# Inverting the first four units' triangles on TensorE by repeated squaring, in a fused recurrence and feed-forward kernel

## The chip, the cores and the metric

The kernel runs on one core of a Trainium2 chip. The metric is the device time of one execution in microseconds, as the median of several executions. The engines of a core are named as the profile names them: PE (TensorE), DVE (VectorE), ACT (ScalarE), POOL (GpSimd) and SP (which issues most transfers).

## What is computed

A recurrence over 768 time steps for 4 x 8 heads of width 40, and then a feed-forward layer with hard-swish over the 3072 tokens of width 320. All data are float32, except that the two weight matrices come as float64.

```python
for t in range(S):
    y[:, :, t] = np.einsum('bhd,bhde->bhe', rt, state)
    Sa = np.einsum('bhde,bhe->bhd', state, at)
    state_decay = state * wt[:, :, None, :] - np.einsum('bhd,bhe->bhde', Sa, bt)
    state = state_decay + np.einsum('bhd,bhe->bhde', vt, kt)
# x: y as (3072 tokens, 320)
h = x @ w_in                                  # 320 -> 2048
g = h * np.clip(h + 3.0, 0.0, 6.0) / 6.0
out = g @ w_out                               # 2048 -> 320
```

The kernel takes time in blocks of 64 steps. A *unit* is one block of two batch entries with their eight heads, so there are 24 units, in *groups* of four (two blocks of the two pairs of batch entries). In a block the recurrence becomes products of matrices, and it needs, for each head, the inverse of a 64 x 64 triangular matrix with ones on the diagonal, made from the products of a and b.

## The kernel before

What matters here is in four parts. Names: `NU` is 4 units, `H` 8 heads, `BL` 64 steps, `L` 32, `NH` = 32 heads of a group.

Preparation of a unit has nine stages: W and gam (decay products), A, B, K (turned and scaled), F (the triangles), factor (`KBt`), E (the masked scores) and EV. A unit's own step has RT, R, VT, S, U, C, UT, rS, sn, H, y and the moves that hand its rows to the feed-forward part.

The inversion of a whole group is done by VectorE on 32 x 32 blocks, in place, with the heads on partitions. It takes 30 rounds of a product and an addition, and the next round needs the one before it.

```python
def invert(F, third, alone=False):
    fb = inv.tile([P, L, L], F32, name="fb")
    nc.vector.transpose(out=fb..., in_=F[:, :, 0:L]...)
    x = inv.tile([P, L, L], F32, name="x", tag="x", bufs=1)
    nc.gpsimd.affine_select(out=x[:], in_=fb[:], ...)
    ...
    for i in range(1, L - 1):
        nc.vector.tensor_tensor(out=pv, in0=..., in1=..., op=ALU.mult)     # prod
        yield
        nc.vector.tensor_tensor(out=rest, in0=rest, in1=pv, op=ALU.add)    # x
        yield
    tb = ...;  nc.vector.transpose(out=tb..., in_=x[:])
    tt = ...;  nc.vector.transpose(out=tt..., in_=x...)
    third.append((F, tb, tt))
```

The third 32 x 32 block of each 64 x 64 inverse is then made on TensorE from `tb`, `tt` and `F`, for two units at a time, and the inverse lies in `tinv`:

```python
def third_block(F, tb, tt, n, first=False):
    for h in range(2 * H):
        for x in range(2):
            nc.tensor.matmul(out=zp[x]..., lhsT=F[...], rhs=tb[...])
    ... # zs <- zp on ScalarE; with first, tinv <- tb on GpSimd
    for h in range(2 * H):
        for x in range(2):
            nc.tensor.matmul(out=tp[x]..., lhsT=tt[...], rhs=zs[...])
    ... # tinv <- tp on ScalarE
```

`U` and `UT` are the first stages that need `tinv`:

```python
def s_U():
    ...
    nc.tensor.matmul(out=up[x]..., lhsT=tinv[half(x), n * H + 4 * s + pr, :], rhs=m["R"]...)
```

The weights arrive as float64 in 20 pieces, and are converted to float32 by VectorE and ScalarE in five steps for each piece. A step is taken each time the generator is advanced; the raw pieces lie in tiles that are not needed yet, among them those of the inversion (`x`, `fb`, `tt`).

```python
def load_weights():
    ...
    for n in range(PIECES + 1):
        nc.vector.tensor_scalar(x, hi, 20, 0x7FF, ...)              # parts
        nc.scalar.activation(out=x, in_=x, func=AF.Relu, ...)       # parts
        yield
        nc.vector.scalar_tensor_tensor(m, raw..., 2.0 ** -52, m, ...)   # of the piece before
        yield
        nc.vector.tensor_tensor(out=out, in0=m, in1=yf, op=ALU.mult)    # win, win2 or wout
        yield
        nc.vector.scalar_tensor_tensor(x, hi, 0x80000000, x, ...)
        yield
        nc.vector.tensor_scalar(hi, hi, 0xFFFFF, 0x4B000000, ...)
        nc.scalar.activation(out=m, in_=m, func=AF.Copy, ...)
        yield
```

The feed-forward part is a stream of jobs, each half of the hidden width for one unit: `expand` (products with `win`, then hard-swish into `gt`) and `contract` (products with `wout`). The first jobs of units 0 and 1 can begin when ten pieces are converted, and all others need all 20:

```python
def available():
    i, r = jobs[0]
    return i in ready and converted[0] >= (PIECES // 2 if i < SPLIT and r == 0 else PIECES)
```

The prelude prepares units 0 to 3 in pairs, starts the inversion of all four at once, advances the weights and some early stages beside it, and then runs the units by a plan:

```python
for t, _ in enumerate(by_twos(0, 4, MIXED, 0, {5: 1, 6: 1, 10: 1})):
    ...
while not third:                 # the inversion of the first group
    aside(1)
    if n % 3 == 1:
        next(weights, None)
    if n % EARLY == 0 and early:
        run(early.popleft())
firsts = [third_block(*third[-1], n, True) for n in (0, 2)]
run(firsts[0]); run(firsts[0], weight=1)
PLAN = """0 U 0 UT 1 R
          0 sn 0 H T
          1 U 1 UT 0 y
          ... """                # T: third block of units 2 and 3
```

After the prelude a steady loop runs the other 20 units, each group with `invert`, `third_block` and the feed-forward jobs in between. The whole kernel:

Of the kernel before, what the change touches and what calls it, by code (L numbers as in the profile page):

```python
# [8 lines left out]
F32 = mybir.dt.float32  # L9
# [7 lines left out]
P = 128  # L17
BL = 64
# [11 lines left out]
def kernel(  # L30
# [111 lines left out]
    mask4 = _ap(mask[:], 0, [[0, 4], [1, BL]])  # L142
    three = const.tile([P, 1], F32, name="three")
# [37 lines left out]
    for name in "BK":  # L181
        others[name] = second(name)
# [44 lines left out]
    def raw_homes():  # L227
# [16 lines left out]
        order = [g, h, a, b, c, d, e, f, a, b, c, d, "x", "fb", "tt", a, b, "fb", "tt", a]  # L244
        free = [None] * 8 + [2, 3, 4, 5, None, None, None, 8, 9, 13, 14, 15]
# [205 lines left out]
    def prepare(i, F):  # L451
# [42 lines left out]
        def b_stage():  # L494
            x = turn_pairs(o["BN"])
            yield PE
            bt = o["bt"] = turned("bt")
            nc.vector.tensor_tensor(out=bt[:], in0=x[:], in1=o["rg"][:], op=ALU.mult)
# [110 lines left out]
    def invert(F, third, alone=False):  # L609
# [26 lines left out]
        if not alone:  # L636
            yield
# [5 lines left out]
        if alone:  # L643
            return
# [6 lines left out]
    def third_block(F, tb, tt, n, first=False):  # L651
# [3 lines left out]
        parts = [slice(0, H), slice(H, 2 * H)] if first else [slice(0, 2 * H)]  # L655
# [8 lines left out]
        for part in parts:  # L664
            for x in range(2):
                z = x * BL
                nc.scalar.activation(out=zs[z:z + L, part], in_=zp[x][z:z + L, part], func=AF.Copy)
        if first:
            for part in parts:
                heads = slice(n * H + part.start, n * H + part.stop)  # L670
                for z in range(0, P, BL):
                    nc.gpsimd.tensor_copy(tinv[z:z + L, heads, 0:L], tb[z:z + L, heads])
                    nc.gpsimd.tensor_copy(tinv[z + L:z + BL, heads, L:BL], tb[z + L:z + BL, heads])
# [9 lines left out]
        for part in parts:  # L683
            heads = slice(n * H + part.start, n * H + part.stop)
            for x in range(2):
                z = x * BL
                nc.scalar.activation(out=tinv[z:z + L, heads, L:BL], in_=tp[x][z:z + L, part],
                                     func=AF.Copy)
# [331 lines left out]
    RFETCH, EARLY, MIXED = 8, 5, 1 / 3  # L1020
    TWOS = 14

    def by_twos(first, steps, mixed, rate, fill={}):
# [3 lines left out]
        for t in range(TWOS):  # L1027
# [8 lines left out]
            if t == 10:  # L1036
                side.append(invert(group_F[-1], third, first == 0))
            yield


    ring.clear()
    ring.extend([("any", 5)] * 5 + [("h", 2)] * 2)
    for name in "WABK":
        for i, engine in enumerate((nc.sync, nc.scalar if name == "W" else nc.sync)):
            fetch(name, i, engine)
    for t, _ in enumerate(by_twos(0, 4, MIXED, 0, {5: 1, 6: 1, 10: 1})):
        if t == 0:
            next(weights)
        limit[0] = {7: 4, 10: 12}.get(t, limit[0])
        while t == 7 and refill[0]():  # L1050
            pass
        if t == RFETCH:
            fetch("R", 0)
    ring.clear()
    ring.append(("any", 5))
    blocks = {}


    stages = [step(i) for i in range(NU)]
    chains = [in_turn(stages[0], ["RT", "VT", "C", "R"]), in_turn(stages[1], ["RT", "VT", "C"])]  # L1060
    early = deque(chains[i] for i in (0, 0, 1, 1, 0, 1, 0))
    n, cleared = 0, []
    while not third:
        aside(1)
        if not third:
            n += 1
            if n % 3 == 1:
                next(weights, None)
            if converted[0] == 2 and not cleared:
                cleared.append(nc.gpsimd.memset(tinv[:], 0.0))  # L1070
# [221 lines left out]
```

## Time and profile before

| | |
|---|---|
| time, median of 3 | 856.66 us (855.93 to 857.93) |
| span of the profiled execution | 853.2 us |
| PE busy | 774.1 us (91%), 15480 instructions |
| DVE busy | 529.4 us (62%), 1032 instructions |
| ACT busy | 310.1 us (36%), 756 instructions |
| POOL busy | 157.5 us (18%), 307 instructions |
| chain that ended last | PE 78%, DVE 12%, issue 3% |

The profile divides the span into 40 slices of 21.3 us and gives the busy share of each engine in each slice as a digit (9 is 90% or more), so that the stages can be told apart. Matmuls of float32 leave two records for each instruction of the program, and transposes leave one. A line of a timeline gives the start, the duration, the engine, the line of the kernel and the operation, and in brackets the idle time before it with what ended it.

### The profile page before, as it was taken

To read this page: it belongs to the slowest core of one execution; us is meant where nothing else is said; L and a number is where in the kernel's file an instruction comes from. 1 tells how busy PE (TensorE), PEld (TensorE's weight loads), DVE (VectorE), ACT (ScalarE), POOL (GpSimd) and SP (SyncE) were. 2 spreads that over 40 slices of the span, in tenths; PEclk is the share of its full clock that TensorE was granted. 3 is DMA by queue.
4 is the path that set the end of the run, shared out by engine and by line. 5 is a ranking of instruction groups with operands and counts; after the bars stand their busy time and mean duration, and the time that the engine had idled before them with its cause. 6 is when DMAs were issued, how large, how long until landed. Compare 5 with 4: busy or idle time off the path is not lost.

```text
span 853.2 us, 34881 instructions
## 1 busy us (share of the span) xinstructions
PE 774.1 (91%) x15480; PEld 660.0 (77%) x15480; DVE 529.4 (62%) x1032; ACT 310.1 (36%) x756; POOL 157.5 (18%) x307
## 2 busy tenths in 40 slices
PE   4723877898999989999999999999999999999998
PEld 3622766776888878888888888888888888888886
DVE  6988598878864579734698454697445674221211
ACT  1322654231344433444324534334453324222111
POOL 3231212112121130221211122113012202000000
PEclk9755878899999999999999999999999999999999
DMA  7572443331123330322231232222232101110000
GB/s 137 86 181 80 112 113 80 64 57 24 33 49 67 59 62 11 61 50 46 46 56 29 43 66 49 45 42 39 41 55 50 18 20 27 25 22 12 17 18 15
DMA packets 174213, 44.99 MB, mean 53 GB/s; under 512 B 157424, under 2 KB 172784, under 8 KB 174064
## 3 DMA queue, kind: packets, MB, share of 16 engines
q1 hardware_dynamic: 171920, 42.44, 26.0%
q8 instruction: 122, 2.00, 1.0%
q10 hardware_dynamic: 2144, 0.33, 0.2%
q14 instruction: 27, 0.22, 0.1%
HBM read 34.08 MB, written 3.93 MB: 45 GB/s over the span
## 4 chain that ended last, share of the span: by engine, by line
PE 78%; DVE 12%; issue 3%; ACT 2%; POOL 1%; DMA 1%; SPq 0%; DVEq 0%; ACTq 0%
PE o L945 24%; PE h L921 20%; PE any L420 6%; PE h L926 5%; PE any L438 3%; PE any L841 3%; PE any L818 3%; DVE prod L626 2%; PE any L660 2%; PE any L679 2%; DVE x L632 2%; PE any L763 2%; PE any L784 1%; PE any L725 1%; PE any L583 1%
## 5 line engine op out<-in xcount | busy, mean ns | idle before, releaser
L945 PE MATMUL o<-wout,gt 128*128 128x320 f32 x768 | 234.8, 449 | 0.0
L921 PE MATMUL h<-xt,win 128*128 128x128 f32 x1536 | 197.6, 283 | 3.2 <-DVE gt L932 3.2
L921 PEld LDWEIGHTS h<-xt,win 128*128 128x128 f32 x1536 | 186.4, 196 | 12.1 <-DVE gt L932 3.9
L945 PEld LDWEIGHTS o<-wout,gt 128*128 128x128 f32 x768 | 139.2, 191 | 54.3 <-issue 1.2
L932 DVE SCALAR_TENSOR_TENSOR gt<-gt,h 128x512 f32<-128x512 f32 x96 | 61.4, 681 | 95.4 <-ACT gt L931 95.4
L931 ACT ACTIVATE gt<-h,three 128x512 f32<-128x512 f32 x96 | 60.8, 684 | 128.0 <-PE h L926 127.8
L856 POOL TENSOR_TENSOR yg<-ys,gam 128x512 f32<-128x512 f32 x24 | 41.3, 1723 | 212.5 <-DVE ys L853 153.9
L626 DVE TENSOR_TENSOR prod<-x 128x30 f32<-128x30 f32 (+9 forms) x180 | 64.1, 356 | 13.4 <-POOL x L617 8.1
L632 DVE TENSOR_TENSOR x<-x,prod 128x30 f32<-128x30 f32 (+9 forms) x180 | 63.9, 355 | 5.5 <-DVE prod L626 0.3
L556 POOL TENSOR_TENSOR KBt<-K,rgt 128x320 f32<-128x320 f32 x24 | 21.6, 899 | 221.6 <-ACT rgt L548 216.3
L926 PE MATMUL h<-xt,win 64*128 64x128 f32 x768 | 55.8, 285 | 0.0
L447 DVE COPY_PREDICATED score<-mask,any 128x256 f32<-128x256 int32 x143 | 53.2, 434 | 1.1 <-PE any L438 1.1
L926 PEld LDWEIGHTS h<-xt,win 64*128 64x128 f32 x768 | 46.6, 187 | 5.2 <-issue 0.3
L474 DVE RECIPROCAL gam<-prods 128x256 f32<-128x256 f32 x24 | 41.5, 1741 | 13.4 <-POOL yg L856 13.1
L825 DVE TENSOR_TENSOR state<-any,state 128x160 f32<-128x160 f32 x48 | 13.3, 319 | 56.0 <-PE any L438 54.5
L489 DVE RECIPROCAL rgam<-prods 128x256 f32<-128x256 f32 x24 | 41.8, 1741 | 0.0
L589 ACT ACTIVATE EV<-any 64x160 f32<-64x160 f32 x92 | 24.8, 295 | 44.4 <-PE any L583 32.6
L463 DVE TENSOR_TENSOR_SCAN prods<-wm,start 128x528 f32<-128x528 f32 x24 | 30.1, 1253 | 16.6 <-ACT wm L460 15.0
L853 DVE TENSOR_TENSOR ys<-any,ys 128x256 f32<-128x256 f32 x44 | 16.6, 418 | 34.5 <-PE any L583 19.9
L704 ACT ACTIVATE RT<-any 128x512 f32<-128x512 f32 x24 | 14.3, 595 | 59.4 <-PE any L420 59.4
L841 PE MATMUL any<-score,KBt 64*64 64x64 f32 x1536 | 31.4, 230 | 2.7 <-DVE score L447 1.6
L841 PEld LDWEIGHTS any<-score,KBt 64*64 64x64 f32 x1536 | 27.3, 142 | 7.6 <-issue 3.3
(184 smaller groups left out, 1137.7 us busy)
## 6 DMA issues: line engine op xcount, KB each, us to landing
B<-in_b_dram SPq DMA_DIRECT2D x48, 80.0 KB
K<-in_k_dram SPq DMA_DIRECT2D x48, 80.0 KB
V<-in_v_dram SPq DMA_DIRECT2D x96, 40.0 KB
out_dram<-ob SPq DMA_DIRECT2D x48, 80.0 KB
R<-in_r_dram SPq DMA_DIRECT2D x92, 40.0 KB
W<-in_w_dram SPq DMA_DIRECT2D x40, 80.0 KB
A<-in_a_dram SPq DMA_DIRECT2D x40, 80.0 KB
xt<-yg SPq DMA_DIRECT2D x72, 40.0 KB
```

The lines of the kernel that those rows point to most:

```text
L420: nc.tensor.transpose(out=o[:, n, :], in_=x[:, 2 * n:2 * n + 2, :].rearrange("p s e -> p (s e)"), identity=ident[:])
L447: nc.vector.copy_predicated(out=x[:, 4 * i:4 * i + 4, :], mask=mask4, data=o[i])
L474: nc.vector.reciprocal(gv[:, :, 0:HB], o["prods"][:, :, 0, 1:HB + 1][:, :, ::-1])
L489: nc.vector.reciprocal(rv[:, :, HB:BL], o["prods"][:, :, 1, 1:HB + 1])
L626: nc.vector.tensor_tensor(out=pv, in0=_ap(x[:], (i + 1) * L + i, [[L, n], [0, i]]), in1=_ap(x[:], i * L, [[0, n], [1, i]]), op=ALU.mult,)
L632: nc.vector.tensor_tensor(out=rest, in0=rest, in1=pv, op=ALU.add)
L841: nc.tensor.matmul(out=y[q][half(s), pr, :], lhsT=o[name][half(q), h * D:h * D + SLOT], rhs=m[name][half(q), 4 * rs + 2 * s + j, :], start ...
L921: nc.tensor.matmul(out=hp[c][:, i, :], lhsT=win[:, t, j * P:(j + 1) * P], rhs=xt[:, t, :], start=(t == 0 and i == 0), stop=False)
L926: nc.tensor.matmul(out=hp[c][:, i, :], lhsT=win2[half(c), (j0 + i) * P:(j0 + i + 1) * P], rhs=xt[half(c), 2, :], start=False, stop=(i == N ...
L931: nc.scalar.activation(out=gt[:], in_=hp[c][:], func=AF.Relu, bias=three[:], scale=1.0)
L932: nc.vector.scalar_tensor_tensor(out=gt[:], in0=gt[:], scalar=6.0, in1=hp[c][:], op0=ALU.min, op1=ALU.mult)
L945: nc.tensor.matmul(out=op[:], lhsT=gts[c][:, n, :], rhs=wout[:, c * HJ + r * NQ + n, :], start=((split or r == 0) and c == 0 and n == 0), ...
```

## The change

The first four units no longer go through `invert` and `third_block`. For a strictly triangular M the inverse is the product (1 + M)(1 + M^2)(1 + M^4)... up to M^32, since M^64 is zero. `by_squares` computes it for two units at a time, with 64 x 64 products in the four quarters of TensorE. Each round squares the power and its transpose, adds the unit matrix to the power (the factor, on GpSimd), and multiplies the sum so far by the factor of the round before. ScalarE empties the powers from PSUM, and VectorE the sums. For it, b is turned with its sign changed, the mask below the diagonal and a unit matrix are prepared, and powers, sums and factors lie in the tiles that `F`, `fb` and `tt` take elsewhere.

The prelude becomes one list: each line names the stages of units, rounds of the squaring (`N0`, `h0`, `N2`, `h2`), steps of the weights (`w`), steps of the feed-forward stream (`f`), limits of loading (`L`), and steps of the second group's preparation (`G`). With it units 0 and 1 run before units 2 and 3 are prepared, and the first feed-forward jobs lie between the rounds of units 2 and 3. Later groups are inverted as before.

The diff, cut to its core:

```diff
-        order = [g, h, a, b, c, d, e, f, a, b, c, d, "x", "fb", "tt", a, b, "fb", "tt", a]
-        free = [None] * 8 + [2, 3, 4, 5, None, None, None, 8, 9, 13, 14, 15]
+        order = [g, h, a, b, c, d, e, f, a, b, c, d, "x", a, b, "fb", "tt", a, b, "fb"]
+        free = [None] * 8 + [2, 3, 4, 5, None, 8, 9, None, None, 13, 14, 15]
...
+            if F is None:
+                nc.vector.scalar_tensor_tensor(bt[:], x[:], -1.0, o["rg"][:], ALU.mult, ALU.mult)
...
+    def by_squares(first):
+        ...
+        def product(o, lhs, rhs):
+            for r in range(4):
+                for h in range(2):
+                    for g in range(2):
+                        at = rhs[half(h)] if len(rhs.shape) == 2 else rhs[half(h), 4 * g + r, :]
+                        nc.tensor.matmul(out=o[h][half(g), r, :], lhsT=lhs[half(h), 4 * g + r, :],
+                                         rhs=at, start=True, stop=True)
+
+        def factor(j):
+            nc.gpsimd.tensor_tensor(out=factors[:, j], in0=powers[:, j, 0], in1=unit8, op=ALU.add)
+
+        for j in range(2):
+            o = data[first + j]
+            for k, (x, y) in enumerate((("at", "bt"), ("bt", "at"))):
+                f = ps_pair(NPR, BL)
+                ...   # 16 products of o[x] and o[y]
+                for s in range(2):
+                    nc.vector.copy_predicated(out=powers[:, j, k, 4 * s:4 * s + 4, :],
+                                              mask=mask4 if k else below4, data=f[s])
+            factor(j)
+        yield
+        for step in range(1, 7):
+            kinds = 2 if step < 5 else 1
+            for j in range(2):
+                if step < 6:
+                    o = ps_pair(kinds, 4, BL)
+                    for k in range(kinds):
+                        product([x[:, k] for x in o], powers[:, j, 1 - k], powers[:, j, k])
+                    found.append(o)
+            o = ps_pair(2, 4, BL)
+            for j in range(2):
+                product([x[:, j] for x in o], factors[:, j], unit if step == 1 else sums[:, j])
+            for j, f in enumerate(found):
+                for b in range(2):
+                    nc.scalar.activation(out=powers[:, j, 0:kinds, 4 * b:4 * b + 4, :], in_=f[b],
+                                         func=AF.Copy)
+                factor(j)
+            for b in range(2):
+                nc.vector.tensor_copy((goal if step == 6 else sums)[:, :, 4 * b:4 * b + 4, :], o[b])
+            yield
...
-    for t, _ in enumerate(by_twos(0, 4, MIXED, 0, {5: 1, 6: 1, 10: 1})):
-        ...
-    while not third:
-        ...
+    PLAN = """0 W 0 gam 1 W 1 gam w1
+              0 A 1 A R0
+              0 B 1 B
+              N0 L4
+              h0 0 K 1 K w2
+              h0 0 factor w2
+              h0 1 factor 0 E 1 E w2 L8
+              h0 0 EV 1 EV w2
+              h0 0 RT 0 VT w2
+              h0 0 C 0 R w2
+              0 U 0 UT w4
+              0 sn 0 H 1 RT w4
+              1 VT 1 C 1 R 0 y w4
+              1 U 1 UT 0 move w4
+              1 sn 1 H 0 move2 w4
+              1 y w4 L12
+              2 W 2 gam 1 move w4
+              3 W 3 gam 1 move2 w4
+              2 A 3 A w6 L15
+              2 B 3 B f2 w3
+              N2 f2 w2
+              h2 2 K 3 K f2 w2
+              h2 2 factor f2 w3
+              h2 3 factor 2 E 3 E f2 w3
+              h2 2 EV 3 EV f2 w3
+              h2 2 RT 2 VT f2 w3
+              h2 2 C L20 f2 w3
+              2 R 2 S f1 w4
+              2 U 2 UT f1 w4
+              2 rS 2 sn 2 H 3 RT f2 w4
+              S 2 y 3 VT 3 C 3 R f2 w4 G
+              3 S 2 move 3 U 3 UT f2 w4 G
+              3 rS 3 sn 3 H 2 move2 f2 w4 G
+              T 3 y G
+              G
+              3 move G
+              3 move2 G"""
```

## The prediction

> **What bounds the kernel now.** I read the slices of the span first, then the busy time by stretch, then the timelines of VectorE and TensorE up to 200 us, and last the groups that give one operation's duration. The slices show where TensorE is not full.
>
> ```profile
> PE   4723877898999989999999999999999999999998
> DVE  6988598878864579734698454697445674221211
> PEclk9755878899999999999999999999999999999999
> ```
>
> A slice is 21.3 us. From the tenth on PE stands at 9 nearly throughout; the first nine, the prelude, are where PE has room, its clock is low, and DVE is the fuller engine. The stretches (us, then busy us and number of instructions on PE, weight load, DVE, ACT, POOL; clock; DMA share; GB/s) put sizes to it:
>
> ```profile
> 7.00:49.00 42.00, 22.32 (x521) 19.04 (x519) 37.67 (x46) 11.15 (x32) 12.60 (x26) 0.83 0.71 127
> 49.00:82.00 33.00, 10.37 (x196) 8.79 (x197) 31.87 (x81) 8.54 (x19) 3.83 (x8) 0.50 0.48 129
> 82.00:128.00 46.00, 35.27 (x1021) 31.47 (x1016) 33.69 (x70) 27.44 (x62) 11.54 (x25) 0.77 0.43 104
> 128.00:162.00 34.00, 26.02 (x444) 21.67 (x445) 29.23 (x46) 11.75 (x26) 7.44 (x11) 0.80 0.37 76
> 162.00:200.00 38.00, 33.67 (x667) 27.55 (x669) 29.20 (x43) 10.84 (x31) 9.83 (x19) 0.98 0.31 53
> 200.00:853.20 653.20, 644.64 (x12640) 549.71 (x12640) 365.45 (x740) 238.21 (x584) 106.73 (x194) 1.00 0.21 39
> ```
>
> After 200 us PE idles 8.6 us in 653. Before 162 us it idles over 60. So the end moves only if the prelude hands over earlier or later to the stretch that PE fills, or if it hands over with more or less PE work already done. From 49 to 82 us DVE runs the inversion of the first four units together with the weight conversion, and everything that needs tinv waits until the two closing transposes:
>
> ```profile
> 40.08 2.13 DVE L614 STREAM_TRANSPOSE fb<-F 128x1024 f32<-128x1024 f32 x1
> ...
> 78.58 1.91 DVE L635 STREAM_TRANSPOSE tb<-x 128x1024 f32<-128x1024 f32 x1
> 80.35 1.97 DVE L640 STREAM_TRANSPOSE tt<-x 128x1024 f32<-128x1024 f32 x1
> ```
>
> The hand-over is visible on PE: the last weight piece is multiplied out on DVE at 158.3 us, and the third feed-forward job (half a unit) begins at 161.64. By then two jobs were expanded and contracted, units 0 to 3 were finished, and W of units 4 to 7 and A of 4 and 5 were turned.
>
> ```profile
> 158.37 1.24 PE L945 MATMUL o<-wout,gt 128*128 128x320 f32 x4
> 159.45 0.60 PE L420 MATMUL any<-ident,W 128*128 128x128 f32 x4
> 161.15 0.66 PE L420 MATMUL any<-ident,WA 128*128 128x128 f32 x4 [1.10 <-ACT wm L460]
> 161.64 1.06 PE L921 MATMUL h<-xt,win 128*128 128x128 f32 x8
> ...
> 544.62 0.68 PE L818 MATMUL any<-V,KBt 64*64 64x40 f32 x32
> 545.11 0.65 PE L818 MATMUL any<-U,KBt 64*64 64x40 f32 x32
> ```
>
> The last two lines give the price of small products: the 32 records are 16 instructions of the program (one unit; a moving fp32 product leaves two records), and group follows group at 0.49 us. Cold they cost twice that.
>
> **What the Trainium skill says.** "TensorE: Matmul & The Clock Gate", Part 1, says the clock is halved until TensorE has been busy for about 3.4 us and again after idling as long. The trace agrees: the mean clock is 0.50 from 49 to 82 us, 1.00 after 200, and four transposes take 1.06 us cold against 0.60 warm. "TensorEngine Tiling (Array Packing)", Performance Considerations, says that packing speeds up the products but not the emptying of PSUM, and that both ScalarE and VectorE should empty it; here 16 packed products take 0.49 us and emptying them is dearer (below). "GPSIMD Engine Reference", section 3.1, finds a two-input elementwise operation on GpSimd about twice as slow as on VectorE; the trace has 1.35 us against 0.63 for 128x512.
>
> **The change part by part.** Durations are from the groups up to 210 us:
>
> ```profile
> L626 DVE TENSOR_TENSOR prod<-x 128x240 f32<-128x240 f32 (+14 forms) x46 | 17.6, 383 | 3.7 <-POOL x L617 2.6
> L491 DVE TENSOR_TENSOR at<-any,gam 128x512 f32<-128x512 f32 x7 | 4.4, 625 | 0.0
> L704 ACT ACTIVATE RT<-any 128x512 f32<-128x512 f32 x4 | 2.3, 587 | 0.0
> L856 POOL TENSOR_TENSOR yg<-ys,gam 128x512 f32<-128x512 f32 x4 | 5.4, 1352 | 36.6 <-ACT ys L851 14.4 <-DMA xt<-yg 11.5 <-DVE ys L853 10.7
> ```
>
> DVE, removed: 60 small operations at about 0.33 us start to start and three transposes of 1.95 us, 25.6 us. Added: per pair of units 8 predicated copies of 0.40 and 12 copies of 128x512 out of PSUM at 0.64 (start to start), twice, 21.8 us. So DVE gains 4 us: nearly everything it gave up it now spends on emptying PSUM.
>
> PE, added: per pair 64 products for the two strict triangles, 4 x 96, 64 and 32, that is 544 instructions, twice 1088, at 0.49/16 us = 33 us warm. Removed: 128 products for F and 256 of the third block, about 8 us. Net +25 us, nearly all before the hand-over.
>
> ACT: 72 us of idle in the prelude take 2 x (16 x 0.59 + 4 x 0.38) = 22 us of new copies, less 10 of F, zs and tinv. POOL: 24 factors at 1.35 to 1.5 us, about 35 us, less 8 of tinv copies.
>
> One round of the squaring (two units): products 2 x 0.98, sum product 0.98, ACT 4 x 0.6, POOL 2 x 1.4, DVE 1.3. Within a round they follow each other, across rounds they overlap in part. By hand, along the order in which each engine gets its instructions:
>
> - First pair: bt is ready at 18.5 us instead of 21 to 22. Six rounds, with the KBt products on POOL and conversion steps between them, take 5 us each: tinv of units 0 and 1 at 50 us, instead of the third block's 85 to 95. DVE has 31 us of work in those 43 and waits 12.
> - Chain of units 0 and 1 (products with tinv, state, y): 50 to 74 us, DVE waiting 5 of them.
> - Units 2 and 3 prepared: 74 to 96 us, DVE full (21 us of work), PE cold and idle.
> - Second pair: PE has N 3.9 us cold, 14 us of products, two jobs expanded (9.3), a contraction (2.3) and 7 us of transposes, E and EV: 36 us without a gap, to 133 us. DVE has 25 us of work in these 37 and waits 12, because each round's copies queue behind feed-forward work on PE.
> - Units 2 and 3 chained, units 4 and 5 prepared, the conversion finished: 38 us of DVE work and some 6 of waits: 177 us.
>
> The same place as a sum. DVE before: scans 7.6, reciprocals 16.9, at/bt/kt 7.4, conversion 55.0, scores 9.6, inversion 25.6, state, gt, ys 7.5: 129.6 us from 7.0, so 136.6; it was 158.3, thus 21.7 of waits. After, up to kt of units 4 and 5, which the third job follows on PE: scans 10.1, reciprocals 20.3, at/bt/kt 11.2, conversion 52.7, scores 9.6, squares 21.8, the rest 8.3: 134 us, so 141 plus waits of 12 + 5 + 0 + 12 + 6 = 35: 176, and the third job at 177 instead of 161.6, 15.4 later. By then PE has done more: B and K turned for 4 and 5 (1.8), two rgam (0.9), F of both (1.9), E of both (1.0): 5.6. Net +9.8: 866.5 us.
>
> I take off 5 for two things. Between 162 and 200 us the old kernel idled 4.3 us on PE, part of it waiting for preparation that DVE has now done by then (W and gam of units 6 and 7); and my waits were counted one queue at a time, though the list of stages was plainly set by hand to fill them. That gives 861 us.
>
> **The rivals.** A: the list does what it was written for. The first pair is through 35 us earlier, so the chain no longer piles up behind the inversion; if the waits stay at the old 22 us, the third job starts at 164, 2 later, and with 5.6 us done early the time is 853; with waits of 12, 843. For it: DVE lost its 60-step chain, and weights and rounds interleave; against it: in-order queues with five engines in each round. B: PE becomes the bound in the second pair's rounds, as above, the jobs woven into it delaying the rounds, and the conversion ends only near 180 us: 866 to 872. For it: the 36 us of PE work counted in one stretch. C: GpSimd's factor sets the rounds; at 1.72 us (its mean over the whole span) two take 3.4 us, still below a round of 5; it would add 3 to 5 us: 865 to 870. D: weight transfers. Pieces in the tiles that the sums and factors occupied can be fetched only after the second pair's last round, and arrive some 5 us later; DVE has 4 us of other work, so this costs 1 to 3 us.
>
> **Range and chances.** B, with the discount, is my centre; A is the optimistic side, weighted nearly as high since a list like this is usually tuned. Range 846 to 875. Faster by over 2% (below 839.5) needs waits under 10 us: 0.09. Slower by over 2% (above 873.8) needs over 45 us: 0.11. The rest 0.80.
>
> **What would show it.** Right: tinv of the first pair at 48 to 53 us; the second pair's last round at 128 to 138 us with PE at 9 tenths in that stretch; the last conversion at 175 to 185 us; third job at 172 to 182; PE busy total near 799 us, and the stretch after the hand-over full as before. Wrong: a third job before 165 us, or PE idling markedly after 180 us, which would mean a new wait in the second group. If the rounds take 7 us or more, POOL or ACT is the bound and not PE.

## The result and the profile after

The changed kernel takes 892.61 us (median of 4 runs, 890.69 to 894.38), against 856.4 us for the kernel before on the same chip: a ratio of 1.042, 95% interval 1.040 to 1.044. It is 4.2% slower. The prediction was 861 us with a range of 846 to 875, and gave "slower by over 2%" a chance of 0.11. The engine that the prediction called full after the prelude is full; it was wrong about the price of a round.

The busy line and the slices of the page after (a slice is now 22.3 us):

```profile
PE 799.6 (90%) x17144; PEld 686.0 (77%) x17144; DVE 530.7 (60%) x1009; ACT 321.9 (36%) x772; POOL 179.7 (20%) x318
...
PE   3765188858899999999999999999999999999998
...
DVE  6358845788885547974378835489643794212211
...
PEclk7798589979899999999999999999999999999999
```

PE's busy time is 799.6 us, where the prediction had "near 799". That agreement is in part chance. The added products (1088) were counted rightly, but not priced rightly: the lines of the rounds (L644) and of their first products (L657) are busy 38.4 and 9.9 us over the whole span, 48.3 where 33 were priced.

```profile
0.00:890.40 890.40, 38.40 (x1920) 35.46 (x1920) 0.95 0.26 51
0.00:890.40 890.40, 9.90 (x256) 8.61 (x256) 0.95 0.26 51
```

What was removed (F and the third block of the first group) was busy 10.0 us, for "about 8"; the rest of PE's work came out some 13 us shorter, and nothing in the prediction says so. PE reaches a steady 9 one slice later than before, and the fifth slice stands at 1. VectorE, at 9 and 8 in these slices before, now stands at 3 in the second slice and at 5 in the third: in the rounds of the first pair it waits.

The stretches by stage (us, then busy us and instructions on PE, weight load, DVE, ACT, POOL; clock; DMA share; GB/s). They are: rounds of units 0 and 1; their chain; preparation of units 2 and 3; rounds of units 2 and 3; two stretches up to the third feed-forward job; the rest.

```profile
17.20:62.50 45.30, 32.23 (x1240) 29.20 (x1240) 20.80 (x38) 15.71 (x36) 19.79 (x21) 0.79 0.58 128
62.50:86.80 24.30, 15.53 (x544) 14.15 (x544) 20.64 (x41) 13.27 (x30) 3.35 (x3) 0.86 0.16 31
86.80:105.80 19.00, 0.00 (x0) 0.00 (x0) 17.54 (x23) 4.36 (x8) 1.79 (x6) 0.52 0.64 141
105.80:157.90 52.10, 43.57 (x1360) 38.90 (x1364) 27.62 (x51) 21.61 (x44) 20.96 (x25) 0.85 0.21 44
157.90:178.90 21.00, 16.50 (x427) 12.52 (x419) 16.40 (x37) 9.10 (x20) 1.47 (x2) 0.94 0.63 159
178.90:207.00 28.10, 18.00 (x495) 15.48 (x493) 25.95 (x32) 8.18 (x22) 9.52 (x17) 0.74 0.36 64
260.00:890.40 630.40, 620.69 (x12463) 530.87 (x12460) 344.42 (x685) 232.74 (x575) 104.30 (x193) 1.00 0.22 39
```

From 260 us to the end PE is busy 98.5% of the time, and in the same stretch of the kernel before 585.41 of 593.20, 98.7%. No new wait entered the second group; the 36 us are lost ahead of it. The two stages of rounds, 45.2 and 52.1 us, are measured from the start of bt to the copies of the finished inverse into tinv, which the timeline of VectorE shows:

```profile
62.45 1.29 DVE L687 COPY tinv<-h 128x512 f32<-128x512 f32 x2 [1.11 <-PE h L644]
```

```profile
157.91 1.29 DVE L687 COPY tinv<-any 128x512 f32<-128x512 f32 x2 [1.31 <-PE any L644]
```

The prediction had these at 50 and 133 us. The third feed-forward job, which it put at 177 and which began at 161.64 before, comes at 207 (timeline of TensorE):

```profile
207.01 1.16 PE L991 MATMUL h<-xt,win 128*128 128x128 f32 x8
```

Set against the prediction's list, stage by stage: tinv of the first pair 12.4 us late; chain and preparation 2.6 us shorter than assumed (43.4 for 46); the second pair's rounds 15.1 longer (52.1 for 37); from there to the third job 5.1 longer (49.1 for 44, of which 3.6 are PE waiting for a transfer of b). The sum is the 30 us by which the job is late. So the question is why rounds whose products were counted rightly take over 40% longer than predicted.

The waits of PE in the first pair's rounds give the first hint (engine, line, what it waited for: us in total, times, longest):

```profile
PE h L657 <- DVE bt L510: 6.8, 1, 6.8
PE h L644 <- issue: 5.9, 4, 2.6
PE any L644 <- issue: 5.3, 3, 2.6
PE h L657 <- DVE mm L662: 0.6, 1, 0.6
```

11.2 us in seven gaps are put down to "issue": PE waited for nothing that the profile shows, in the middle of groups of products (L644) whose operands were there. No copy of ScalarE and no factor of GpSimd ends these gaps. They can be placed by counting PE's matmul records from the start of the kernel, and set beside the packets of the queue that the page calls "q8 instruction", from the raw records of the same trace:

```
gap ends at   length   matmul records so far      packet of q8 (16,384 bytes) begins
   43.33       1.24         729                        44.39
   47.61       1.45         857                        48.81
   51.46       1.75         985                        53.68
   56.35       2.58        1110                        59.43
```

The gaps lie 128 matmul records apart (the trace lacks a few records), and a packet begins 1.1 to 3.1 us after PE goes on. A float32 product of these leaves two matmul records and two weight loads, so 128 records are 64 products or 256 instructions of TensorE. The page's DMA queues say the same. Before:

```profile
q8 instruction: 122, 2.00, 1.0%
```

After:

```profile
q8 instruction: 135, 2.21, 1.1%
```

13 packets more, and 17144 - 15480 = 1664 matmuls and as many weight loads more: 3328 instructions, 13 times 256. TensorE gets its program in blocks of 256 instructions, and in the rounds it stands still between one block and the next.

In the second pair that wait is nearly absent:

```profile
PE any L657 <- DVE bt L510: 22.2, 1, 22.2
PE any L644 <- ACT mm L683: 2.6, 2, 2.2
PE any L657 <- DVE mm L662: 2.1, 2, 1.6
PE any L644 <- issue: 1.1, 1, 1.1
PE h L991 <- DVE gt L1002: 1.1, 1, 1.1
```

The first line is the idle stretch ahead of the stage. The other four sum to 7 us, and PE is busy for 43.6 of the 52.1, so the second pair needed another explanation than the first.

### The profile page after: what moved, and what is told of

The parts are those of the page before. It is cut to its first block, busy times and chain, and to the rows that moved or that the text cites. A ratio compares the mean times of both kernels' runs of the same rounds, so it can differ in the third digit from the quotient of the medians.

```text
span 890.4 us, 38248 instructions
## 1 busy us (share of the span) xinstructions
PE 799.6 (90%) x17144; PEld 686.0 (77%) x17144; DVE 530.7 (60%) x1009; ACT 321.9 (36%) x772; POOL 179.7 (20%) x318
## 4 chain that ended last, share of the span: by engine, by line
PE 68%; DVE 7%; issue 2%; ACT 1%; POOL 1%; DVEq 0%
PE o L1015 21%; PE h L991 18%; PE h L996 5%; PE any L431 5%; PE any L449 3%; PE any L888 2%; PE any L911 2%; DVE x L715 1%; DVE prod L709 1%; PE any L739 1%; PE any L795 1%; PE any L833 1%; PE any L751 1%; PE any L870 1%; PE any L597 1%
## 5 line engine op out<-in xcount | busy, mean ns | idle before, releaser
L1015 PE MATMUL o<-wout,gt 128*128 128x320 f32 x768 | 231.0, 448 | 0.0
L991 PE MATMUL h<-xt,win 128*128 128x128 f32 x1536 | 195.2, 282 | 1.9 <-DVE gt L1002 1.9
L991 PEld LDWEIGHTS h<-xt,win 128*128 128x128 f32 x1536 | 183.4, 194 | 10.2 <-DVE gt L1002 2.9
L1015 PEld LDWEIGHTS o<-wout,gt 128*128 128x128 f32 x768 | 141.8, 193 | 56.6 <-issue 2.7
L709 DVE TENSOR_TENSOR prod<-x 128x30 f32<-128x30 f32 (+9 forms) x150 | 55.0, 367 | 11.8 <-POOL x L700 6.9
L715 DVE TENSOR_TENSOR x<-x,prod 128x30 f32<-128x30 f32 (+9 forms) x150 | 54.2, 361 | 4.7
L458 DVE COPY_PREDICATED score<-mask,any 128x256 f32<-128x256 int32 x140 | 52.1, 434 | 1.7 <-PE any L449 1.5
L996 PEld LDWEIGHTS h<-xt,win 64*128 64x128 f32 x768 | 46.9, 187 | 4.7 <-issue 0.3
L648 POOL TENSOR_TENSOR factors<-mm,extra 128x512 f32<-128x512 f32 x24 | 30.1, 1270 | 68.1 <-PE any L644 32.6
L800 DVE TENSOR_TENSOR RR<-any,EV 128x160 f32<-128x160 f32 x44 | 12.2, 318 | 35.1 <-PE any L449 35.1
```

What stands on the lines that cost most here:

```text
L458: nc.vector.copy_predicated(out=x[:, 4 * i:4 * i + 4, :], mask=mask4, data=o[i])
L709: nc.vector.tensor_tensor(out=pv, in0=_ap(x[:], (i + 1) * L + i, [[L, n], [0, i]]), in1=_ap(x[:], i * L, [[0, n], [1, i]]), op=ALU.mult,)
L991: nc.tensor.matmul(out=hp[c][:, i, :], lhsT=win[:, t, j * P:(j + 1) * P], rhs=xt[:, t, :], start=(t == 0 and i == 0), stop=False)
L996: nc.tensor.matmul(out=hp[c][:, i, :], lhsT=win2[half(c), (j0 + i) * P:(j0 + i + 1) * P], rhs=xt[half(c), 2, :], start=False, stop=(i == N ...
L1015: nc.tensor.matmul(out=op[:], lhsT=gts[c][:, n, :], rhs=wout[:, c * HJ + r * NQ + n, :], start=((split or r == 0) and c == 0 and n == 0), ...
```

## The experiments

Each is the changed kernel with one edit, or with several of the same edits together. The theories at the start: F, TensorE is held by the supply of its instructions; W, conversion steps stand in ScalarE's queue ahead of the copies of the rounds; L, the way of a round through ScalarE, GpSimd and their semaphores sets its length; and, for the second pair, the woven feed-forward (FFN) steps and the cold clock. The lengths are those of the two stages of rounds; "second group" is the start of the scan that opens the preparation of unit 4. Before and after:

```profile
141.64 1.26 DVE L463 TENSOR_TENSOR_SCAN prods<-wm,start 128x528 f32<-128x528 f32 x1 [1.23 <-ACT wm L460]
178.89 1.26 DVE L474 TENSOR_TENSOR_SCAN prods<-wm,start 128x528 f32<-128x528 f32 x1 [1.26 <-ACT wm L471]
```

The ratio is to the kernel before on the same chip.

| kernel | time, us | ratio to before, 95% | first pair | second pair | second group | span |
|---|---|---|---|---|---|---|
| before | 856.4 | | | | 141.6 | 853.2 |
| after | 892.6 | 1.042 (1.040 to 1.044) | 45.2 | 52.1 | 178.9 | 890.4 |
| e1, no conversion in the rounds | 904.9 | 1.058 (1.054 to 1.061) | 45.2 | 48.2 | 190.8 | 902.3 |
| e2, no FFN steps in the rounds | 892.9 | 1.044 (1.041 to 1.046) | 44.0 | 40.6 | 182.6 | 891.2 |
| e3, no rounds | 847.4 | 0.990 (0.987 to 0.993) | 19.6 | 31.5 | 134.9 | 846.3 |
| e4, repeated products at the end | 998.4 | single run | 45.0 | 50.6 | 177.2 | 996.7 |
| e5, half of the products | 878.8 | 1.029 (1.027 to 1.030) | 33.6 | 48.7 | 167.8 | 879.5 |
| e6, warm start of the second pair | 892.0 | 1.044 (1.042 to 1.046) | 45.2 | 52.1 | 178.7 | 888.8 |
| e7, later loads | 891.0 | 1.042 (1.040 to 1.044) | 46.4 | 51.7 | 179.8 | 889.2 |
| p1, another order of the list | 922.0 | 1.078 (1.076 to 1.081) | 47.8 | 58.5 | 171.5 | 918.1 |
| e8, half, no FFN | 885.6 | 1.035 (1.031 to 1.039) | 34.2 | 39.3 | 172.8 | 883.3 |
| e9, half, no FFN, warm | 884.1 | 1.034 (1.030 to 1.037) | 33.9 | 39.0 | 175.2 | 883.6 |
| e10, half, warm | 877.3 | 1.026 (1.023 to 1.030) | 33.4 | 46.9 | 166.2 | 875.6 |
| e11, half, no FFN, no conversion, warm | 886.9 | 1.037 (1.031 to 1.043) | 34.1 | 31.5 | 176.0 | 884.2 |

The lengths come from one execution each. Up to its end e4 is the changed kernel without an edit, and its second pair takes 50.6 us instead of 52.1; so a difference of about 1.5 us between two kernels in that column tells nothing.

**Conversion steps out of the rounds (e1).** They are done in the lines that follow. Pieces 0 and 1 lie raw in tinv's tiles, are converted late, and are overwritten by the inverse; a part of the weights is therefore not the reference's, at the same amount of work.

```diff
-              h0 0 K 1 K w2
-              h0 0 factor w2
+              h0 0 K 1 K
+              h0 0 factor
...                                # likewise in all lines with N2, h0 and h2
-              0 U 0 UT w4
+              0 U 0 UT w8
```

> The conversion steps are taken out of the rounds of both pairs and done in the lines after them; the rounds keep all else. In the changed kernel the first pair takes 45 us (from the start of the first bt to the copies into tinv) and the second 52. Theory W (a conversion step's ScalarE half stands in front of the emptying of the powers, and waits for a VectorE half that stands behind the sums): first pair 33 to 36 us, second 42 to 45. Theory F (TensorE waits for its own instructions, which come in blocks of 256, one product being four of them): first pair 41 us or more with the same gaps of 1 to 3 us every 128 records, second 48 or more. Time under both within 1% of the changed kernel, since the steps are only moved.

Measured: the first pair stays at 45.2 us and PE's "issue" gaps in it at 11.1 us (6.9 + 4.2). As the cause of the first pair W falls. The second pair is shorter by 3.9 us, about half of what W expected there; it comes back below (e9, e11). The conversion ends later, and the time rises by 12 us, 1.4%, more than the 1% that was allowed for.

**FFN steps out of the second pair's rounds (e2).**

```diff
-              h2 2 K 3 K f2 w2
-              h2 2 factor f2 w3
+              h2 2 K 3 K f0 w2
+              h2 2 factor f0 w3
...                                # likewise in all lines from "2 B 3 B" to "h2 2 C"
-              2 R 2 S f1 w4
+              2 R 2 S f6 w4
```

> The feed-forward steps are taken out of the second pair's rounds and done in the lines after them. Theory P (the rounds wait behind feed-forward work on TensorE): second pair 52 us to 36 to 39, no gaps inside the groups of products. Theory F (instructions): the pair holds some 2500 TensorE instructions, ten blocks, so 40 to 45 us at about 4 us for a block, and gaps inside the groups now show as they do in the first pair. Theory W: 48 us or more.

Measured: the second pair falls from 52.1 to 40.6 us, by the 11.5 us that the woven jobs cost it, into the range of F. The gaps for issue in it are 2.4 us in four, against 10.4 in the first pair of the same kernel, which has the same products. The two stages, first and second pair, differ in what else is transferred (the last two figures, DMA share and GB/s):

```profile
17.50:61.60 44.10, 31.61 (x1240) 28.58 (x1240) 21.45 (x37) 15.99 (x36) 19.77 (x21) 0.81 0.58 131
104.80:145.40 40.60, 31.83 (x1274) 28.51 (x1274) 26.64 (x48) 17.68 (x39) 20.71 (x24) 0.81 0.24 51
```

The time does not move: the jobs are then done in the lines that follow, and the second group begins 3.7 us later.

**No rounds (e3).** Rounds 1 to 5 are left out and the last multiplies the first factor by the unit matrix, so tinv is not an inverse.

```diff
-        for step in range(1, 7):
+        for step in (0, 0, 0, 0, 0, 6):
+            if not step:
+                yield
+                continue
...
-                product([x[:, j] for x in o], factors[:, j], unit if step == 1 else sums[:, j])
+                product([x[:, j] for x in o], factors[:, j], unit)
```

> Rounds 1 to 5 of both pairs are left out, and the last multiplies the first factor with the unit matrix, so the inverse is left wrong; everything else stays. All theories: the time of the rounds beyond the work that lies beside them comes off; first pair 15 to 20 us instead of 45, second 22 to 28 instead of 52, time 830 to 845 us. If the time stays above 870, the rounds are not what the kernel lost its time to.

Measured: 847.4 us, just above the range. Rounds 1 to 5 of the two pairs cost 45 us of the time; and without them this list is only 1% ahead of the kernel before. The first pair takes 19.6 us, as expected, but the second 31.5 and not 22 to 28: what is woven into its lines fills that much without the rounds.

**Repeated products at the end (e4).** Four stretches of 512 products of 64x64 tiles with no operand to wait for and results that nobody reads, in turn over 64 and 128 columns.

```diff
+    for cols in (BL, P, BL, P):
+        for n in range(8):
+            o = [ps_any([P, 512]) for _ in range(2)]
+            for r in range(16):
+                for h in range(2):
+                    for g in range(2):
+                        nc.tensor.matmul(out=o[h][half(g), (r % 4) * P:(r % 4) * P + cols],
+                                         lhsT=ident[half(h), half(g)], rhs=ident[half(h), 0:cols],
+                                         start=True, stop=True)
```

> The changed kernel with four stretches of 512 products added at its end, with 64, 128, 64 and 128 columns, back to back, no reader and no other work (their results are not used). Theory F: the 64-column stretches take as long as the 128-column ones or nearly, about 30 us each (8 blocks at some 4 us), with gaps every 128 records. If instructions are no limit: 16 us for 64 columns (0.031 us for one) and about 30 for 128, without gaps.

The timeline of TensorE in these stretches:

```profile
890.96 2.09 PE L1338 MATMUL any<-ident 64*64 64x64 f32 x128 [1.65 <-issue]
894.43 2.09 PE L1338 MATMUL any<-ident 64*64 64x64 f32 x128 [1.38 <-issue]
897.90 2.09 PE L1338 MATMUL any<-ident 64*64 64x64 f32 x128 [1.38 <-issue]
901.38 2.09 PE L1338 MATMUL any<-ident 64*64 64x64 f32 x128 [1.38 <-issue]
905.12 2.30 PE L1338 MATMUL any<-ident 64*64 64x64 f32 x128 [1.65 <-issue]
909.14 28.95 PE L1338 MATMUL any<-ident 64*64 64x128 f32 x1024 [1.72 <-issue]
```

This is F in pure form. 64 products (x128 records, 256 instructions) run in 2.09 us, 0.033 us each, just as priced; then PE stands 1.4 to 1.65 us, and the next 64 begin 3.5 to 3.7 us after the last: 0.056 us a product. Over 128 columns 512 products run for 28.95 us without a gap, 0.057 us each. Twice the columns cost nothing. The page's instruction queue grows from 135 to 167 packets, 32 for 2 x 4096 instructions. The Trainium skill, "Runtime: NRT & Kernel Launch", section "Instruction fetch mechanics", says that instructions are refilled in blocks of 16 KiB, 256 instructions, the next fetched while the current one runs, and that the cost is "mostly hidden". The block size agrees with these runs; that it is hidden does not, for a run of products short enough: a block lasts them 2.1 us, and the next takes 3.5.

**Half of the products of the rounds (e5).** Each product takes the columns of two heads, so that half as many instructions stream the same columns. Odd heads are multiplied by their neighbour's matrix: what comes out is not the inverse.

```diff
-            for r in range(4):
+            for r in (0, 2):
...
-                        nc.tensor.matmul(out=o[h][half(g), r, :], lhsT=lhs[half(h), 4 * g + r, :],
-                                         rhs=at, start=True, stop=True)      # at: 64 columns
+                        nc.tensor.matmul(out=o[h][half(g), r:r + 2, :], lhsT=lhs[half(h), 4 * g + r, :],
+                                         rhs=at, start=True, stop=True)      # at: 2 x 64 columns
```

> Half of the products of the rounds, each over the columns of two heads (128 instead of 64); the odd heads are multiplied by their neighbour's matrix, so what is computed is no inverse, and the same columns are streamed by half the instructions. Theory F (TensorE is held by the supply of its instructions, a block of 256 every 3.5 to 3.7 us): the rounds of the first pair shrink from 45 us (bt to the copies into tinv) to 32 to 36, those of the second from 52 to 42 to 46, and the time falls to about 868 to 877. Rival L (the way of a round through ScalarE, GpSimd and their semaphores): as many copies and factors as before, so 45 and 52 stay within 2 us and the time stays near 892. Rival M (the columns streamed at the granted clock): no change either.

The waits of PE in the first pair's rounds of this kernel:

```profile
PE h L658 <- DVE bt L510: 7.3, 1, 7.3
PE any L449 <- ACT VT L807: 4.1, 1, 4.1
PE h L645 <- POOL factors L649: 1.8, 2, 1.0
PE any L645 <- issue: 0.8, 1, 0.8
```

The gaps for issue fall from 11.2 to 0.8 us and the first pair by the same, from 45.2 to 33.6, while copies, factors and semaphores are as many as before. So F is shown for the first pair, and L falls there. (The wait for VT belongs to the chain after the rounds.) The second pair loses only 3.4 us, less than the 6 to 10 expected, and the time, 878.8 us, lies just above the expected range.

**A warm start of the second pair (e6).** Twenty matmuls of 128x512 stand ahead of `N2`.

```diff
-              N2 f2 w2
+              D20 N2 f2 w2
...
+            elif kind == "D":
+                for _ in range(int(count)):
+                    x = ps_any([P, 512])
+                    nc.tensor.matmul(out=x[:], lhsT=ident[:], rhs=start[:, 0:512], start=True, stop=True)
```

> Twenty matmuls of 128x512 with results that nobody reads stand ahead of the second pair's first step, in the 22 us in which TensorE idles. Theory C (a cold clock at the start of the second pair costs some 4 us there): second pair 52 to about 48 us, time 887 to 889. If the clock is no cause: second pair 52, time 892 to 893.

Measured: second pair 52.1 and the time 892.0, no change. The stretch from bt to the first copies of a sum, in the changed kernel and here, shows that the clock did rise, from 0.62 to 0.76:

```profile
105.80:122.10 16.30, 12.21 (x336) 11.23 (x336) 6.92 (x16) 3.46 (x6) 3.79 (x3) 0.62 0.43 102
105.60:120.10 14.50, 11.29 (x338) 10.05 (x337) 6.82 (x16) 3.17 (x6) 2.80 (x3) 0.76 0.49 115
```

It is 1.8 us shorter, and the next rounds give that back. So theory C, a cold start that costs this stage some 4 us, falls.

**Later loads (e7).** Weight pieces 4 to 7 are loaded after the first pair's rounds, so that their transfers are not beside those of the instructions.

```diff
-              h0 1 factor 0 E 1 E w2 L8
+              h0 1 factor 0 E 1 E w2
...
-              0 U 0 UT w4
+              L8 0 U 0 UT w4
```

> The loads of weight pieces 4 to 7 are issued after the first pair's rounds and not within them. Theory T (the weight transfers slow the transfers of the instruction blocks, which come every 4.9 to 5.4 us late in the first pair against 3.6 in the repeated products): first pair 45 to 42 or 43 us, time 889 to 891. If the blocks are slow of themselves: 45 us and 892 to 893.

Measured: 46.4 us and 891.0, no gain in the stage. But the edit hardly changed what is transferred in it: 0.56 of the DMA engines' time and 125 GB/s, against 0.58 and 128 in the changed kernel.

```profile
17.00:63.40 46.40, 32.94 (x1240) 30.26 (x1240) 20.84 (x37) 15.69 (x36) 20.23 (x21) 0.76 0.56 125
```

So these four pieces are not what makes the blocks late; whether the other transfers of the stage do is not tested. That e2's second pair, at 0.24, has gaps of 2.4 us where its first, at 0.58, has 10.4 is a hint that they do, and no proof.

**Another order of the list (p1).** Units 2 and 3 are prepared beside the rounds of units 0 and 1, and their rounds stand beside the chain of 0 and 1; the FFN steps come after.

```diff
-              h0 0 K 1 K w2
-              h0 0 factor w2
+              h0 0 K 1 K 0 factor 2 W w2
+              h0 1 factor 2 gam w2
...
-              N2 f2 w2
-              h2 2 K 3 K f2 w2
+              N2 0 sn 0 H 1 RT w6 L12
+              h2 1 VT 1 C 1 R 0 y w6
...
+              f2 2 RT 2 VT w6
```

> The same arithmetic in another order of the list: units 2 and 3 are prepared beside the rounds of units 0 and 1, their rounds stand beside the chain of units 0 and 1, and the FFN steps come after. Theory F leaves TensorE's rounds at 45 us each but fills the idle stretches of VectorE in the first and of TensorE between 80 and 106: the third FFN job begins at 180 to 190 instead of 207, time 862 to 875. Theory L (the lines of the list are full, each as long as its longest chain): the lines grow by what is put into them, and the time stays at 885 to 900.

Measured: 922 us, worse than every expectation. The pairs take 47.8 and 58.5 us and not 45 each. The rounds of both are through at 128.9 us instead of 157.9 and the second group begins 7.4 us earlier, but from 300 to 700 us PE is busy 91 to 97% of each 100 us, where in the changed kernel it is 96 to 100%. Over the whole span PE waits like this:

```profile
PE h L991 <- DMA xt<-yg: 17.5, 6, 4.3
PE any L644 <- issue: 17.4, 11, 2.0
PE h L991 <- DVE gt L1002: 9.4, 3, 6.0
```

The first line is new, and the third was 1.9 us in the changed kernel: feed-forward jobs reach PE before their input has arrived. That the lines of feed-forward work, moved back, no longer keep a distance from what they read is my reading of it; no run separates it.

**Half of the products and no FFN steps (e8).** The edits of e5 and e2 together.

> Half of the products of the rounds, each over two heads' columns (no inverse), and the FFN steps of the second pair's lines moved behind its rounds. Theory F plus weave: of the second pair's 52.1 us, instruction supply and the FFN steps are all that lies above the predicted 36.5 less the FFN steps' own work; with both away it falls to 33 to 36 us, as the first pair with half of the products (33.6). Rival K (the cold clock, or the coupling of ScalarE and VectorE, holds the rest): 38 to 41 us. The time is of no weight, as the FFN steps come later: 870 to 880.

Measured: second pair 39.3 us, as rival K said, and only 1.2 less than with the FFN steps out alone, which is not clear of chance. Something else still holds it.

**The same with a warm start (e9).** The edit of e6 added.

> As the run before, with twenty 128x512 matmuls of no use ahead of the second pair. With half of the products TensorE's clock can bind again, so a cold start costs here: second pair 2 to 4 us shorter than in the run without them, 31 to 33 us. If the clock holds nothing: the same within 1 us.

Measured: 39.0 us; the clock is not the rest either. The timelines of e9 show what is. TensorE in the third round:

```profile
117.13 0.39 PE L645 MATMUL any<-sums,factors 64*64 64x128 f32 x4
119.70 1.75 PE L645 MATMUL any<-sums,factors 64*64 64x128 f32 x28 [2.19 <-ACT mm L684]
```

ScalarE at the same time:

```profile
115.44 0.44 ACT L562 ACTIVATE rgt<-any 128x320 f32<-128x320 f32 x1 [0.32 <-PE any L559]
117.45 0.66 ACT L339 ACTIVATE wout<-wout 128x512 f32<-128x512 f32 x1 [1.57 <-DVE wout L336]
118.44 0.72 ACT L312 ACTIVATE parts<-parts,low 128x512 uint32<-128x512 uint32 x1 [0.34 <-DVE parts L310]
119.07 2.04 ACT L684 ACTIVATE mm<-any 128x512 f32<-128x512 f32 x4
```

The four copies of the powers (L684) stand in ScalarE's queue behind two conversion steps (L339, L312), each of which waits for VectorE, which has its own queue. The products done by 117.3 are not emptied before 119, and PE waits 2.19 us for it. Over the whole second pair of e9 PE waits 4.4 us for these copies, in three times, and for nothing else there longer. This is W, in the second pair.

**Half of the products, FFN steps in place, warm start (e10).** The edits of e5 and e6.

> Half of the products, the FFN steps where they were, and the twenty matmuls of no use ahead of the second pair: second pair 48.1 to 45 us if the cold clock holds part of it, time 875 to 878; 48 us and 879 if not.

Measured: 46.9 us and 877.3. The length lies nearer to the second outcome, the time in the range of the first; the intervals of the times with and without the matmuls overlap. Nor are the 1.8 us to e5 clear of chance, and they are not where the matmuls act: from bt to the first copies of a sum it is 13.8 us against 14.1, and the rest lies in the last two rounds, where the clock was 0.87 and 0.89 in e5 and 1.00 here. That the warm start did this is not shown.

**Conversion steps out as well (e11).** e9 with the `w` of the lines from `N2` to `h2 2 C` moved behind them.

```diff
-              D20 N2 f0 w2
-              h2 2 K 3 K f0 w2
+              D20 N2 f0
+              h2 2 K 3 K f0
...
-              2 R 2 S f6 w4
+              2 R 2 S f6 w13
```

> As the run with half of the products, no FFN steps and the matmuls of no use, and now the 15 conversion steps of the second pair's lines also moved behind its rounds. In that run ScalarE twice idled 1.6 to 3.7 us ahead of a conversion step and TensorE then waited about 2 us for the copies behind it. Theory W2 (the conversion steps hold back ScalarE's copies in the second pair's rounds): 39.0 falls to 34 to 35 us, the length of the first pair with half of the products. Rival: 38 to 39 us as before. The time is of no weight.

Measured: 31.5 us, 7.5 less than e9, more than expected, and below the first pair's 34. From the first copies of a sum to tinv the stretch of this kernel reads:

```profile
110.50:129.70 19.20, 18.74 (x552) 16.43 (x553) 9.52 (x17) 11.31 (x28) 15.92 (x19) 1.00 0.15 25
```

PE is busy 98% of it, at full clock: five rounds in 19.2 us, 3.8 us each. Here PE's own work is the bound. From 52.1 us, taking out the FFN steps gives 40.6, halving the instructions as well 39.3 (39.0 warm), and taking out the conversion steps as well 31.5. The 11.5 and the 7.5 us are clear of chance, the 1.2 of the halving is not. The order matters: halving gives 3.4 us alone, and taking out the conversion steps 3.9 alone and 7.5 as the last of the three. That in each round the slowest of the three hides the others is my reading. And e11 takes away the steps' work together with their place in the queues; that it is the place rests on the timelines and the 4.4 us of e9.

## Why the prediction was wrong

**The step that failed, first pair.** "Six rounds, with the KBt products on POOL and conversion steps between them, take 5 us each: tinv of units 0 and 1 at 50 us." The product price behind it, 0.49 us for 16, came from a group of 16 products with other work around it, and inside a block it is right: e4's products run there at 0.033 us. But a round has 96 of them in a row, 384 instructions, one and a half blocks of 256, and e4 shows such a block every 3.5 to 3.7 us: 1.5 blocks are 5.4 us and not the 3 us priced. The mis-sized term is "at 0.49/16 us = 33 us warm" for 1088 products: where nothing else stands between them they cost 0.056 us, 61 us. In the changed kernel they keep PE busy for 48.3 us, a low clock included, and 12.3 us of gaps for issue stand between them. (The prediction's "256 of the third block" are matmul records; the products removed there are 128, so net 832 were added, which is the 1664 records above.) With half of the instructions the first pair takes 33.6 us, against the 31.5 (18.5 to 50) that the prediction had: the rest of its mechanism for the first pair held.

**The step that failed, second pair.** "36 us without a gap, to 133 us". The gaps were there: 8.5 us of the 52.1, and 43.6 us busy where 36 were counted (a group's busy time includes what a low clock stretches, and the clock was 0.85). Rival B said that the jobs woven into the rounds delay them, and that is the largest part, 11.5 us; it was sized at 866 to 872, since it priced the work and not the waits. A round's copies stand behind conversion steps and gt on ScalarE and VectorE, in order, and the next round's products behind those. The prediction spoke of DVE's waits there (12 us); the conversion steps (19 in these lines; e11's 15 is a miscount) it counted among DVE's work, though two of every five also hold a place in ScalarE's queue. That costs 3.9 us with all else in place and 7.5 with nothing else in the way.

**What was to tell, and told wrongly.** "If the rounds take 7 us or more, POOL or ACT is the bound and not PE." They take 4 to 9 us, and POOL is not it: in e5, with the factors untouched, PE waits 1.8 us for them in the first pair. Rival C falls. ACT it is in part, in the second pair, by its queue and not by its work (busy 21.6 us of 52.1). Instruction supply was on no list. The group of the factors, from the page after (busy us, mean ns of one, then idle time before it), shows 24 of 1.27 us, 30 us in all, a little under the price:

```profile
L648 POOL TENSOR_TENSOR factors<-mm,extra 128x512 f32<-128x512 f32 x24 | 30.1, 1270 | 68.1 <-PE any L644 32.6
```

**What held.** The chain of units 0 and 1, "50 to 74 us", took 24.3 us; the preparation of units 2 and 3, "DVE full, PE cold and idle", 19.0 with VectorE busy 17.5 and PE at nothing, though the two were together 2.6 us shorter; PE's sum of 799, though by errors that cancel. Work done earlier than before was credited with 5.6 us; the third job came 45.4 us later and the time is 36.2 us longer, so it was 9.2.

**The discount.** "I take off 5 for two things." Neither shows. In the table the span less the start of the second group is 711.6 us before and 711.5 after, and 708 to 712 in every experiment that ran that far but p1 (e4 has work added at the end). What comes after the hand-over took the same time in all of them, and the list was not better set than the hand count but worse.

**Rival A**, the list as it was meant to work, failed at its own condition: e3, with no rounds to wait for, lies at 847, in the range that A gave, 843 to 853. Rival D, weight transfers: e7 shifted four pieces without gain; those after the second pair, which D was about, were not tried alone.

**What stays open.** Why a block takes 3.5 us when its packet takes 0.9 to 1.5 us; why the gaps for issue are 11.2 us in the first pair and nearly absent in the second, for which the other transfers are an untested candidate (e2, e7); and what would become of rounds with fewer, wider products that still compute the inverse. e5 bounds that: 878.8 us, or 877.3 warm, with the FFN and conversion steps where they are, still 2.6 to 2.9% above the kernel before. No version here beats it but the one that leaves the rounds out.

## What to carry to other kernels

Price a run of small products by TensorE's instructions as well as by columns: four for each float32 product, and here 256 instructions every 3.5 to 3.7 us in products that would run faster (e4); doubling the columns of a product, from 64 to 128, was free. Work that is woven between the rounds of a dependent chain costs its place in every in-order queue that it passes, not only its time on the engine where it is counted; to find such causes, take them out together as well as singly, as each hides the others. And where one point hands over to a full engine, follow that point: here the span was its time plus 710 us.

## What the runs showed of the hardware that I had not expected

A dense run of 64x64 float32 products over 64 columns is no faster than one over 128: 0.056 and 0.057 us a product. TensorE's instructions come in blocks of 256 (13 packets of 16,384 bytes for 3328 instructions more), and between blocks it stood 1.4 to 1.65 us in the repeated products and up to 2.6 us in the first pair. The page shows this only as "issue" in the middle of a group, with PE's own busy share reading as an engine with room (32 us of 45).
